# A fused top-k attention and feed-forward kernel: later transposes of a first head, earlier requests for the first low weights, more weight bits in the output banks, and new planner numbers

## The chip, the cores and the metric

The kernel runs on one core of one Trainium2 chip. The metric is the device time of one execution in microseconds (us), the median of the runs shown. Its engines are PE (TensorE, matrix products, with PEld for its weight loads), DVE (VectorE), ACT (ScalarE), POOL (GpSimd) and SP, whose queue issues the transfers (SPq in the rows).

## The reference

```python
# 8 batches, 8 heads, 576 positions, 64 wide
scores = q @ k.T / sqrt(64)
kth = np.partition(scores, -32, axis=-1)[..., -32:-31]      # 32nd largest of each row
scores = np.where(scores >= kth, scores, -1e9)
attn = softmax(scores)                                       # with 1e-9 added to the sum
x = (attn @ v).transpose(0, 2, 1, 3).reshape(4608, 512)
h = x @ w_in                                                 # 512 x 2048
P = a0 + a1*h + a2*h**2 + a3*h**3
Q = 1 + |b0|*|h| + |b1|*h**2
out = (P / (Q + 1e-6)) @ w_out                               # 2048 x 512
```

`w_in` and `w_out` are given with 64 bits, the rest with 32.

## The kernel before

**Attention.** The work is cut into 288 tiles. A tile is 128 query rows of one head against all 576 keys; a main unit is two such tiles, the two heads of a pair `hp` (there are four pairs, 0 to 3) at one block of rows, and the last 64 rows of both heads of a pair make one mixed tile. For a tile PE makes the scores `s` (`scores`, lines 706, 711 and 715), ACT copies them to `sb` (`evacuate`, 722), DVE folds the two halves into `hi` and `lo` and works through the largest values with MAX8 and MATCH_REPLACE8 (733 to 752), ACT makes the exponentials `e` (783), and DVE makes the masked product `pr` (`probs`, 786). PE then transposes `pr` (`trp`, 863) with the reciprocal sums `rw` (865), ACT copies the transposes to `p` (875), PE multiplies them with the values (`av`, 889), and ACT and POOL write the scaled result to `x_m` (906, 908). In `add_values`, `t0` and `t1` are the masked products of a unit's first and second head; transpose 0 needs only `t0`, transposes 1 and 2 need `t1`.

**Exact products from halves.** Most products are made of a high part and a low part of each operand. For the keys of a head pair this means one load `kl`, a high part `kh`, a low part, and four copies by the SP queue into `ka` and `kb` (606); for the queries one load `qx`, the two parts, and a stack of six copies into `q` (655, 657). Head pair 0 of batch 0 is "plain": its keys and queries are used as they are loaded (711).

**Feed-forward.** 256 rows of x are a chunk, 18 chunks in all, each of 8 groups. A group makes 24 products `ph` of 256 columns (1036) from `xh`, `xl`, the resident high weights `win_h` and the low weights `wi`, 512 KB that the SP queue fetches anew for each group (`load_wi`, 1044). ACT, POOL and DVE form the rational function, and 12 products `po` of 512 columns (1182) add to the output with `wout` and the low weights `wl` (1193). Names carry the batch or chunk: `wi_m_0_0` belongs to a main chunk.

**Weights.** In the first 230 us the 64-bit weights are also turned into high and low parts, 32 blocks of 512 columns. Each block takes two PSUM banks for its bits one after the other (lines 421 to 433): for blocks 0 to 7 of the two "o" banks, later the accumulators of `po`, for the others of the two "mm" banks, which the transposes, `av` and `ph` use as well.

**What sets the order.** `Plan` is a list scheduler that runs when the program is built. Every step has a priority key (smaller first), a length, the steps it waits for and the buffers it takes; keys are a tile's number times `T` plus an offset from the table `KEY` (for instance `AV` for `av`, `PT` for transposes, `WL` for the fetches of low weights). On the chip every engine and the SP queue then run their instructions strictly in the order that the plan wrote down, each waiting for its own semaphores.

Of the kernel before, what the change touches and what calls it, by code (L numbers as in the profile page):

```python
# [10 lines left out]
F32 = mybir.dt.float32  # L11
# [6 lines left out]
AX = mybir.AxisListType  # L18
PSUM = bass.MemoryType.PSUM

KEY = {'STAY': 0.0, 'WH': ('ACT', 'POOL'), 'XH': ('POOL',), 'TH': 0, 'EU': 4.119, 'SC': 0, 'HW': 256, 'Q0': ('POOL', 'ACT'), 'Q1': ('POOL',), 'SPLIT': (0, 1, 2, 3, 4, 5, 6, 7), 'XS': 1, 'P1': ('ACT', 'POOL'), 'P3': ('ACT', 'POOL'), 'RH': ('POOL',), 'p2': ('POOL', 'DVE'), 'p4': ('POOL',), 'ratio': ('POOL', 'DVE'), 'ratio_low': ('POOL',), 'URG': -100.0, 'PT': -10.303, 'AV': 2.038, 'MOE': 125.127, 'QT': -12.596, 'KT': -22.066, 'EL': 1.0, 'LOOK': 0.27, 'T': 5.448, 'KL': -16.348, 'KH': -8.844, 'PJ': 101.114, 'WL': 0.96, 'EX': 8.711, 'EW': 9.121, 'ALT': {'ACT': 0.388, 'DVE': 29.071, 'POOL': 0}, 'WG': 5.531, 'QL': -17.951, 'QH': 0.956, 'PACE': 15.382, 'B4': 0, 'RT': 1.0, 'WI': 0, 'WO': 0, 'MS': 0.313, 'NM': ('POOL', 'ACT'), 'WD': ('ACT',), 'LP': ('POOL',), 'FL': ('DVE',), 'VL': -15.549, 'RI': 7.085, 'ROOM': {'s': 1, 'e': 1, 'mm': 2, 'o': 2, 'k': 4, 'kr': 1, 'km': 2, 'q': 2, 'qr': 1, 'v': 2, 'sb': 3, 'lo': 1, 'hi': 2, 'pr': 2, 'p0': 1, 'p1': 1, 'p2': 1, 'm': 3, 'u': 4, 'rw': 1, 'fl': 2, 'x': 2, 'xm': 1, 'xs': 1, 't': 14, 'ob': 4, 'wi': 2, 'wl': 4}, 'TN': 2, 'IL': 0.996, 'SLACK': {'DVE': 0.0, 'PE': 0.0, 'ACT': 0.0, 'POOL': 0.0}, 'CF': 5.0, 'LD': 1.5, 'CL': 1.0, 'C0': 6.0, 'ML': 0.431, 'GL': 0.285}
NEG = -3.0e38
NB = 8

# [12 lines left out]
class Plan:  # L37
# [11 lines left out]
    BACK = 0.17  # L49
    CHANGE = 0.085  # L50
    SPARE = 2
    CLOCK = ((150.0, 1.2), (300.0, 1.05))

    def __init__(self, room):
        self.ring = {t: [-1.0] * n for t, n in room.items()}
# [134 lines left out]
def tile_topk_attention__then__rational_ffn(  # L190
# [10 lines left out]
    nc = tc.nc  # L201
# [31 lines left out]
    def add(*args, **kwargs):  # L233
        return plan.add(*args, **kwargs)
# [322 lines left out]
    def add_weights(key0, gap):  # L557
        n = 0
        blocks = []
        for e in range(0, DFF, 512):  # L560
            for c in range(HP):
                away = [win_l[e // 256 + i][:, c] for i in range(2)]
                split = (win_h[:, c, e : e + 512], None, away)
                tags = ["xs"] if c == HP - 1 and e < DFF // 2 else ["t"] * 3
                blocks.append((("i", c, e // 512), w_in, c * P, e, split, tags))
            for f in range(4 * (e // 512), 4 * (e // 512) + 4):
                split = (wout[f], None, [wout_l[f]] if f in wout_l else None)
                tags = ["t"] * (3 if f // FG in SPLIT else 2)
                blocks.append((("o", f), w_out, f * P, 0, split, tags))
        for n, (name, *args) in enumerate(blocks):  # L570
            bits = name[2] >= 4 - KEY["WI"] if name[0] == "i" else name[1] >= 16 - KEY["WO"]
            w_steps[name] = weight_block(*args, key0 + n * gap, f"w{n}", bits, "o" if n < 2 * HP else "mm")

    def add_kv(bi, hp, index, key):
        nm = f"{bi}_{hp}"
        kv = Obj()
        kv.index, kv.nm = index, nm
        kv.khold, kv.mhold = Hold("k", 2 * NJ), Hold("km")  # L580
        rhold = Hold("kr")
        kv.plain = index == 0

        def load_plain():
            kv.x = buf(kv.khold, [P, S], F32, f"ka_{nm}", "a")
            nc.sync.dma_start(kv.x, qk[index][:, 0:S])

        def load():
            kv.low = buf(rhold, [P, S], F32, f"kl_{nm}", "l")
            nc.sync.dma_start(kv.low, qk[index][:, 0:S])  # L590

        def high_part():
            kv.high = buf(rhold, [P, S], F32R, f"kh_{nm}", "h")
            affine(kv.high, kv.low, 1.0, 0.0)

        def low_part():
            engine().tensor_tensor(
                out=kv.low.bitcast(F32R), in0=kv.low, in1=kv.high.bitcast(F32), op=ALU.subtract
            )

        def stack():
            kv.k = [buf(kv.khold, [P, S], F32R, f"k{x}_{nm}", f"{x}") for x in "ab"]
            top, end = slice(0, D), slice(D, P)
            high, low = kv.high.bitcast(F32), kv.low
# [23 lines left out]
    def add_q(u):  # L628
        kv, key, pair = u.kv, u.key, u.pair
        n = len(pair.units) * P  # L630
        nm = f"{kv.nm}_{u.j}"
        q = pair.q = Obj()
        q.hold, rhold = Hold("q", 2 * len(pair.units)), Hold("qr")

        def load_plain():
            q.x = buf(q.hold, [P, 2, 2, 2 * P], F32, f"q_{nm}")[:, 0, 0]
            nc.sync.dma_start(q.x[:, 0:n], qk[kv.index][:, S + u.j * P :][:, 0:n])

        def load():
            q.x = buf(rhold, [P, 2, 2 * P], F32R, f"qx_{nm}")  # L640
            nc.sync.dma_start(q.x[:, 1, 0:n].bitcast(F32), qk[kv.index][:, S + u.j * P :][:, 0:n])

        def high_part():
            affine(q.x[:, 0, 0:n], q.x[:, 1, 0:n].bitcast(F32), 1.0, 0.0)

        def low_part():
            x = q.x.bitcast(F32)
            engine().tensor_tensor(out=q.x[:, 1, 0:n], in0=x[:, 1, 0:n], in1=x[:, 0, 0:n], op=ALU.subtract)

        def stack():  # L650
            q.q = buf(q.hold, [P, 2, 2, 2 * P], F32R, f"q_{nm}")
# [179 lines left out]
    def add_values(u):  # L831
# [190 lines left out]
    def add_group(x, o, g, key, split, xs, oholds):  # L1022
# [210 lines left out]
    def build():  # L1233
# [167 lines left out]
```

## Time and profile before

| what | value |
|---|---|
| runs of the kernel | 1501.80, 1502.86, 1498.61 us (median 1501.8) |
| the profiled execution | 1500.79 us, of which the span is 1498.9 us |
| busy share of the span | PE 93%, DVE 90%, ACT 85%, POOL 80% |
| mean granted TensorE clock | 0.965 of full |
| transfers | 301.57 MB, 201 GB/s on average |

Busy shares are averages over stages with different limits: at the start DVE works alone at speed, then PE and DVE are both nearly full, and at the end DVE has nothing left. So the stages have to be read one by one.

### The profile page before, as it was taken

What the parts mean: (1) busy time and instruction counts of PE and PEld (TensorE: products, weight loads), DVE (VectorE), ACT (ScalarE), POOL (GpSimd) and SP (SyncE); (2) the same over time, 40 slices, a digit from 0 to 9 for tenths busy, and PEclk for the clock granted to TensorE, in tenths of its full rate; (3) what the DMA queues carried; (4) which work ended last, traced back from release to release, by engine and by line L of the source; (5) the groups of instructions that cost most, each with busy time, mean ns of one, the idle gap of its engine ahead of it and who ended that gap; (6) DMA issues with size and microseconds to landing.
All of it is one profiled execution on the core that took longest, in us unless ns stands there. A gap on an engine that the chain in (4) does not pass through costs nothing.

```text
span 1498.9 us, 32412 instructions
## 1 busy us (share of the span) xinstructions
PE 1400.6 (93%) x9729; PEld 1178.6 (79%) x9729; DVE 1356.2 (90%) x4567; ACT 1274.5 (85%) x2592; POOL 1197.0 (80%) x1776
## 2 busy tenths in 40 slices
PE   5467789999999899999999999999999999999997
PEld 3345567878888788888888888888888788888886
DVE  7998999999999899999999999999999999999100
ACT  7776998989897798988898899899889798989664
POOL 6986889788877687888787788689777798877896
PEclk9656899999999999999999999999999999999999
DMA  7767885667765777567755676667765766564464
GB/s 227 230 202 220 239 253 179 195 182 215 233 198 144 221 207 237 166 203 226 222 184 174 213 235 200 195 192 221 216 205 151 241 204 223 157 197 144 142 219 135
DMA packets 173690, 301.57 MB, mean 201 GB/s; under 512 B 26048, under 2 KB 79296, under 8 KB 173504
## 3 DMA queue, kind: packets, MB, share of 16 engines
q1 hardware_dynamic: 173504, 299.39, 64.7%
q8 instruction: 80, 1.31, 0.4%
q14 instruction: 106, 0.87, 0.2%
HBM read 229.64 MB, written 18.87 MB: 166 GB/s over the span
## 4 chain that ended last, share of the span: by engine, by line
PE 74%; DVE 8%; ACT 6%; POOL 5%; issue 3%; DMA 2%; SPq 1%; POOLq 0%; ACTq 0%; DVEq 0%
PE ph_m L1036 21%; PE po_m L1182 19%; PE av L889 10%; PE s L715 8%; PE trp L863 7%; PE ph_t L1036 3%; DVE m L744 3%; PE po_t L1182 2%; DVE hi L752 2%; PE s L706 2%; DVE pr L786 1%; DMA wi_m<-win_l 1%; ACT p L875 1%; ACT sb L722 1%; PE trp L865 1%
## 5 line engine op out<-in xcount | busy, mean ns | idle before, releaser
L744 DVE MAX8 m<-hi 128x8 f32<-128x288 f32 (+1 forms) x1152 | 500.5, 452 | 0.4
L752 DVE MATCH_REPLACE8 hi<-m,hi 128x288 f32<-128x288 f32 x864 | 379.1, 443 | 0.0
L1036 PE MATMUL ph_m<-xh_m,win_h 128*128 128x256 f32 x1024 | 306.8, 300 | 4.6 <-ACT p L875 2.8
L1036 PE MATMUL ph_m<-xh_m,wi_m 128*128 128x256 f32 x1024 | 291.4, 285 | 6.3 <-DMA wi_m<-win_l 6.3
L1036 PE MATMUL ph_m<-xl_m,win_h 128*128 128x256 f32 x1024 | 289.8, 283 | 0.0
L875 ACT COPY p<-trp 128x512 f32<-128x512 f32 (+1 forms) x448 | 227.3, 513 | 43.1 <-PE trp L863 29.7
L863 PE MATMUL trp<-ident,pr 128*128 128x128 f32 x1312 | 224.0, 283 | 37.6 <-ACT w_w L433 20.6
L722 ACT COPY sb<-s 128x576 f32<-128x576 f32 x288 | 184.5, 641 | 59.3 <-PE s L715 37.5
L783 ACT ACTIVATE e<-sb,st 128x576 f32<-128x576 f32 x288 | 216.8, 753 | 18.9 <-DVE pr L786 15.4
L786 DVE SCALAR_TENSOR_TENSOR pr<-sb,m,e 128x576 f32<-128x576 f32 x288 | 229.7, 798 | 1.7 <-ACT e L783 1.0
L1092 POOL TENSOR_TENSOR pa_m<-pa_m,va_m 128x512 f32<-128x512 f32 x128 | 165.1, 1291 | 75.9 <-ACT va_m L1089 70.4
L863 PEld LDWEIGHTS trp<-ident,pr 128*128 128x128 f32 x1312 | 164.6, 145 | 72.9 <-ACT w_w L433 27.4
L1182 PE MATMUL po_m<-wout,g_m 128*128 128x512 f32 x512 | 218.2, 426 | 0.2
L1182 PE MATMUL po_m<-wl_m,g_m 128*128 128x512 f32 x512 | 202.4, 395 | 4.0 <-DMA wl_m<-wout_l 3.3
L1036 PEld LDWEIGHTS ph_m<-xh_m,win_h 128*128 128x128 f32 x1024 | 195.0, 190 | 13.4 <-ACT p L875 8.2
L1182 PE MATMUL po_m<-wout,gl_m 128*128 128x512 f32 x512 | 202.2, 395 | 2.5 <-POOL gl_m L1098 2.5
L1036 PEld LDWEIGHTS ph_m<-xh_m,wi_m 128*128 128x128 f32 x1024 | 194.6, 190 | 7.4 <-DMA wi_m<-win_l 7.4
L1036 PEld LDWEIGHTS ph_m<-xl_m,win_h 128*128 128x128 f32 x1024 | 195.3, 191 | 1.9
L889 PE MATMUL av<-p,vm 128*64 128x256 f32 (+1 forms) x1920 | 188.2, 345 | 3.8 <-ACT p L875 2.0
L1111 POOL TENSOR_TENSOR pa_m<-pa_m,hh_m 128x512 f32<-128x512 f32 x128 | 165.3, 1291 | 16.4 <-ACT hh_m L1117 6.5
L1098 POOL TENSOR_TENSOR gl_m<-pa_m,g_m 128x512 fp32r<-128x512 f32 x128 | 165.2, 1291 | 7.2 <-PE po_t L1182 3.0
L889 PEld LDWEIGHTS av<-p,vm 128*64 128x64 f32 x1920 | 112.2, 143 | 73.1 <-issue 17.7
(117 smaller groups left out, 3202.9 us busy)
## 6 DMA issues: line engine op xcount, KB each, us to landing
wl_m<-wout_l SPq DMA_DIRECT2D x256, 256.0 KB, 3.4
wi_m<-win_l SPq DMA_DIRECT2D x128, 512.0 KB, 4.1
vm<-in_v_dram SPq DMA_DIRECT2D x96, 320.0 KB, 3.1
q<-qx SPq DMA_DIRECT2D x124, 128.0 KB, 2.7
q<-qx SPq DMA_DIRECT2D x248, 64.0 KB, 2.1
km<-in_qk_dram SPq DMA_DIRECT2D x32, 352.0 KB, 3.7
kl<-in_qk_dram SPq DMA_DIRECT2D x31, 288.0 KB, 4.0
w_w<-in_moe_w_in_dram SPq DMA_DIRECT2D x32, 256.0 KB, 3.9
```

Of the source, the lines that this page charges most:

```text
L722: nc.scalar.copy(t.sb, t.s[:, :, 0:HF])
L744: nc.vector.max(to, t.both if not full and o == 24 else getattr(t, src))
L752: nc.vector.match_replace(x, t.m[:, o : o + 8], x, NEG)
L783: nc.scalar.activation(t.e, t.sb, AF.Exp, scale=SCALE, bias=t.st)
L786: nc.vector.scalar_tensor_tensor(out=t.pr, in0=t.sb, scalar=t.kth, in1=t.e, op0=ALU.is_ge, op1=ALU.mult, accum_out=u.ss[:, t.h : t.h + 1],)
L863: nc.tensor.transpose(u.ps[i][:, c * P : (c + 1) * P], u.pr[:, x], ident)
L875: nc.scalar.copy(pair.pT[i][:, at].rearrange("p c n -> p (c n)"), u.ps[i][:, 0 : n * P])
L889: nc.tensor.matmul(pair.av[d, 0 : u.nq * len(pair.units)], lhs, x[:, 0, d] if u.mixed else x[:, 0] if lone else x, start=(c == 0), stop=(c ...
L1036: nc.tensor.matmul(y.ph[:, f * NT : (f + 1) * NT], w, z[:, c, :], start=(c == 0 and i == 0), stop=(c == HP - 1 and i == 2),)
L1098: engine().tensor_tensor(out=tile_("gl", F32R), in0=y.pa, in1=y.g.bitcast(F32), op=ALU.subtract)
L1111: nc.gpsimd.tensor_tensor(out=x, in0=x, in1=z, op=ALU.mult)
L1182: nc.tensor.matmul(o.po[i], z, w, start=(ff == 0 and n == 0), stop=(ff == NF - 1 and n == 2),)
```

## The change

The table `KEY` gets new numbers and four pieces of code change. The numbers that the prediction speaks of: `AV` 2.038 to 4.464 and `PT` -10.303 to -7.135 (`av` and transposes yield more to scores), `WL` 0.96 to 21.38 (fetches of low weights yield more), `EX` 8.711 to 14.43, `EW` 9.121 to 19.62, `T` 5.448 to 5.373, `PACE` 15.38 to 17.42, `WG` 5.531 to 5.914 (time between weight blocks); `XH` lets ACT as well as POOL make high parts. New entries are `OB` 16, `K0` 50.97 and `W0` 108.17. The diff of the code:

```diff
-    CLOCK = ((150.0, 1.2), (300.0, 1.05))
+    CLOCK = ((150.0, 1.5), (210.0, 1.1))
...
-            w_steps[name] = weight_block(*args, key0 + n * gap, f"w{n}", bits, "o" if n < 2 * HP else "mm")
+            w_steps[name] = weight_block(*args, key0 + n * gap, f"w{n}", bits, "o" if n < KEY['OB'] else "mm")
...
-        kv.plain = index == 0
+        kv.plain = False
...
-        if kv.plain:
-            kv.load = add("SP", dma(1, P * S), load_plain, key=k2, take=[kv.khold])
-            return kv
+        if index == 0:
+            raw = Obj()
+            raw.khold, raw.plain = kv.khold, True
+            kv.first = raw
+            kv.khold.users = 4
+            raw.load = add("SP", dma(1, P * S), load_plain, key=k2, take=[kv.khold])
+            kv.khold = Hold("k", 2 * NJ - 4)
+            k2 += KEY['K0']
...
             for h, here, there in ((0, top, end), (1, end, top)):
-                nc.sync.dma_start(x[here, :, h, 0:n], y[here, :, 0:n])
-                for i in range(2):
-                    nc.sync.dma_start(x[there, i, h, 0:n], y[here, 1 - i, 0:n])
+                for rows in (here, there):
+                    nc.sync.dma_start(x[rows, :, h, 0:n], y[here, :, 0:n])
...
-        u, kv, key = t.u, t.u.kv, t.key
+        u, key = t.u, t.key
+        kv = u.kv.first if u.plain else u.kv
...
-            dep = [t0 if i == 0 else t1]
+            dep = [t1]
...
-        wi = add("SP", dma(1, P * 1024), load_wi, wdep + split[0:1], key + KEY['WL'], take=[wih])
+        wi = add("SP", dma(1, P * 1024), load_wi, wdep + (split[0:1] if x.n or g > 1 else []), key + KEY['WL'] - (KEY['W0'] if x.n == 0 else 0), take=[wih])
...
+            u.plain = n < 2
```

So transpose 0 waits for the second head's masked product too; the stack of queries takes four copies in place of six (the same bytes); the bits of blocks 8 to 15 use the "o" banks; the first chunk's low weights are asked for earlier, in the first two groups without waiting for the chunk itself; and only the first two units are plain, so head pair 0 of batch 0 loads its keys a second time and splits them.

How the new plan moves instructions is seen in three places. The first is PE's queue from the first tile of head pair 1 on (`s_0_1_0`); before it reads

```order
L715 MATMUL s_0_1_1_408<-kb_1_258,q_1_0_210 128x288 x4
L863 MATMUL trp_0_1_0_427<-ident,pr_1_0_300 128x128 x4
L863 MATMUL trp_0_1_0_461<-ident,pr_1_0_300 128x128
L865 MATMUL trp_0_1_0_461<-ident,rw_1_0_455 128x128
L889 MATMUL av_1_0_472<-p_0_0_0_235,vm_0_0_131 64x256
...
L889 MATMUL av_1_0_472<-p_0_0_0_342,vm_0_0_131 64x256 x2
L715 MATMUL s_1_1_0_514<-ka_1_257,q_1_0_210 128x288 x4
L863 MATMUL trp_0_0_1_524<-ident,pr_0_1_433 128x128 x4
```

and in the changed kernel

```order
L720 MATMUL s_0_1_1_398<-kb_1_231,q_1_0_269 128x288 x4
L868 MATMUL trp_0_1_0_425<-ident,pr_1_0_337 128x128 x4
L868 MATMUL trp_0_1_0_434<-ident,pr_1_0_337 128x128 x4
L868 MATMUL trp_0_1_0_470<-ident,pr_1_0_337 128x128
L870 MATMUL trp_0_1_0_470<-ident,rw_1_0_461 128x128
L720 MATMUL s_1_1_0_482<-ka_1_230,q_1_0_269 128x288 x4
L894 MATMUL av_1_0_494<-p_0_0_0_301,vm_0_0_131 64x256
...
L894 MATMUL av_1_0_494<-p_0_0_0_333,vm_0_0_131 64x256 x2
L720 MATMUL s_1_1_1_552<-kb_1_231,q_1_0_269 128x288 x4
```

The next tile's scores `s_1_1_0` now stand ahead of the block `av`, and both large transposes of a unit stand together behind its second head's scores.

The second is the SP queue around the fetch of `wi` for the fifth chunk (`wi_m_0_0`), some 490 us into the span; before

```order
L674 DMA vm_1_2_7119<-in_v_dram 128x640
L655 DMA q_2_2_7136<-qx_2_2_6972 64x2x256
L657 DMA q_2_2_7136<-qx_2_2_6972 64x256 x2
L655 DMA q_2_2_7136<-qx_2_2_6972 64x2x256
L657 DMA q_2_2_7136<-qx_2_2_6972 64x256 x2
L606 DMA ka_0_7181<-kh_0_5610 64x576
...
L606 DMA kb_0_7182<-kh_0_5610 64x576
L641 DMA qx_3_2_7216<-in_qk_dram 128x256
L1044 DMA wi_m_0_0_7221<-win_l_98 128x1024
```

and in the changed kernel

```order
L678 DMA vm_1_2_7101<-in_v_dram 128x640
L661 DMA q_2_2_7113<-qx_2_2_6942 64x2x256 x4
L606 DMA ka_0_7149<-kh_0_5509 64x576
...
L606 DMA kb_0_7150<-kh_0_5509 64x576
L646 DMA qx_3_2_7188<-in_qk_dram 128x256
L1198 DMA wl_m_2_7_1_7191<-wout_l_121 128x512
L1049 DMA wi_m_0_0_7203<-win_l_98 128x1024
```

The stack is two copies shorter, and a `wl` fetch now stands between it and `wi`.

The third is PE's queue where the first chunk's products begin; before

```order
L711 MATMUL s_3_0_0_1622<-ka_0_129,q_0_2_775 128x288 x2
...
L865 MATMUL trp_0_4_3_1675<-ident,rw_4_3_1611 128x128
L1036 MATMUL ph_m_0_0_1683<-xh_m_0_1415,win_h 128x256
L1036 MATMUL ph_m_0_0_1683<-xl_m_0_1416,win_h 128x256
```

and in the changed kernel

```order
L720 MATMUL s_3_0_1_1674<-kb_0_624,q_0_2_1006 128x288 x4
...
L720 MATMUL s_2_1_0_1755<-ka_1_230,q_1_2_1231 128x288 x4
L868 MATMUL trp_0_2_0_1776<-ident,pr_2_0_1577 128x128
L870 MATMUL trp_0_2_0_1776<-ident,rw_2_0_1761 128x128
L1041 MATMUL ph_m_0_0_1815<-xh_m_0_1388,win_h 128x256
L1041 MATMUL ph_m_0_0_1815<-xl_m_0_1389,win_h 128x256
```

The first `ph` moved behind two further score tiles (`s_3_0_1` and `s_2_1_0`). Counted over the whole queue, PE has this many `ph` and `po` ahead of a tile (before / changed): ahead of tile 32, 72 and 12 / 27 and 12; of tile 40, 138 and 48 / 105 and 33; of tile 64, 423 and 165 / 408 and 168; of tile 96, 768 and 375 / 768 and 369; of tile 240, 2496 and 1209 in both; behind the last `av`, 312 and 225 / 333 and 219.

## Rows read from the trace of the kernel before

**Rows 1.** The page: span, busy time and share with instructions, TensorE clock in tenths.
```profile
span 1498.9 us, 32412 instructions
PE 1400.6 (93%) x9729; PEld 1178.6 (79%) x9729; DVE 1356.2 (90%) x4567; ACT 1274.5 (85%) x2592; POOL 1197.0 (80%) x1776
PEclk9656899999999999999999999999999999999999
```

**Rows 2.** Busy time by stretch, with granted clock, share of transfers, GB/s.
```profile
core 0: us, PE busy (x) PEld busy (x) DVE busy (x) ACT busy (x) POOL busy (x), PEclk, DMA share, GB/s
0.00:100.00 100.00, 55.16 (x201) 34.69 (x202) 86.60 (x288) 75.71 (x190) 79.81 (x165) 0.77 0.71 220
100.00:163.00 63.00, 45.77 (x237) 29.67 (x235) 55.63 (x182) 47.28 (x119) 45.73 (x77) 0.64 0.73 224
163.00:200.00 37.00, 30.10 (x210) 24.76 (x208) 36.02 (x123) 34.41 (x76) 34.13 (x46) 1.00 0.80 235
501.00:1390.00 889.00, 880.86 (x6410) 757.24 (x6409) 878.03 (x2963) 789.40 (x1568) 713.06 (x1045) 1.00 0.65 201
1390.00:1498.90 108.90, 101.17 (x622) 88.54 (x620) 2.72 (x11) 67.81 (x113) 87.42 (x88) 0.98 0.53 168
```

**Rows 3.** Timeline of DVE: start, length, what, idle before it and its releaser.
```profile
7.45 0.46 DVE L733 TENSOR_TENSOR hi<-s,sb 128x288 f32<-128x288 f32 x1 [7.45 <-ACT sb L722]
...
17.45 0.46 DVE L733 TENSOR_TENSOR hi<-s,sb 128x288 f32<-128x288 f32 x1 [0.70 <-ACT sb L722]
...
40.95 0.46 DVE L733 TENSOR_TENSOR hi<-s,sb 128x288 f32<-128x288 f32 x1 [2.00 <-ACT sb L722]
...
64.43 0.46 DVE L733 TENSOR_TENSOR hi<-s,sb 128x288 f32<-128x288 f32 x1 [1.03 <-ACT sb L722]
...
88.43 0.46 DVE L733 TENSOR_TENSOR hi<-s,sb 128x288 f32<-128x288 f32 x1 [0.41 <-ACT sb L722]
...
140.92 0.46 DVE L733 TENSOR_TENSOR hi<-s,sb 128x288 f32<-128x288 f32 x1 [1.32 <-ACT sb L722]
```

**Rows 4.** Timeline of PE in the start: `av` ahead of scores, split and plain scores.
```profile
34.41 4.54 PE L889 MATMUL av<-p,vm 128*64 128x256 f32 x20
...
86.39 1.33 PE L715 MATMUL s<-ka,q 128*128 128x288 f32 x4
...
137.93 2.29 PE L711 MATMUL s<-ka,q 64*128 64x288 f32 x4
```

**Rows 5.** Waits, 0 to 165 us: engine, for whom, us in total, times, longest.
```profile
PE trp L863 <- ACT w_w L433: 16.1, 9, 3.0
```

**Rows 6.** Waits of PE, 165 to 1400 us.
```profile
PE ph_m L1036 <- DMA wi_m<-win_l: 6.3, 4, 2.9
...
PE po_m L1182 <- DMA wl_m<-wout_l: 3.3, 2, 1.7
```

**Rows 7.** Timeline of the SP queue ahead of one late `wi` (issue times).
```profile
482.24 0.33 SPq L674 DMA_DIRECT2D vm<-in_v_dram  x1
483.00 0.62 SPq L655 DMA_DIRECT2D q<-qx  x1
483.67 1.24 SPq L657 DMA_DIRECT2D q<-qx  x2
...
485.61 1.25 SPq L657 DMA_DIRECT2D q<-qx  x2
...
490.10 0.45 SPq L1044 DMA_DIRECT2D wi_m<-win_l  x1
```

**Rows 8.** Timeline of PE: the product that waited for this `wi`.
```profile
494.75 0.58 PE L1036 MATMUL ph_m<-xh_m,wi_m 128*128 128x256 f32 x1 [2.86 <-DMA wi_m<-win_l]
```

**Rows 9.** Busy time of the stretch behind that wait, columns as in rows 2.
```profile
494.00:501.00 7.00, 6.25 (x29) 6.23 (x30) 4.76 (x17) 1.96 (x5) 2.25 (x4) 0.51 0.73 253
```

**Rows 10.** The chain that ended last, its end: start, us, what.
```profile
1426.45 9.79 PE po_m L1182 x42
...
1444.75 5.76 PE ph_m L1036 x48
```

More of the change, by code (lines that the diff above doesn't have):

```diff
@@ L19 @@
 PSUM = bass.MemoryType.PSUM
-KEY = {'STAY': 0.0, 'WH': ('ACT', 'POOL'), 'XH': ('POOL',), 'TH': 0, 'EU': 4.119, 'SC': 0, 'HW': 256, 'Q0': ('POOL', 'ACT'), 'Q1': ('POOL',), 'SPLIT': (0, 1, 2, 3, 4, 5, 6, 7), 'XS': 1, 'P1': ('ACT', 'POOL'), 'P3': ('ACT', 'POOL'), 'RH': ('POOL',), 'p2': ('POOL', 'DVE'), 'p4': ('POOL',), 'ratio': ('POOL', 'DVE'), 'ratio_low': ('POOL',), 'URG': -100.0, 'PT': -10.303, 'AV': 2.038, 'MOE': 125.127, 'QT': -12.596, 'KT': -22.066, 'EL': 1.0, 'LOOK': 0.27, 'T': 5.448, 'KL': -16.348, 'KH': -8.844, 'PJ': 101.114, 'WL': 0.96, 'EX': 8.711, 'EW': 9.121, 'ALT': {'ACT': 0.388, 'DVE': 29.071, 'POOL': 0}, 'WG': 5.531, 'QL': -17.951, 'QH': 0.956, 'PACE': 15.382, 'B4': 0, 'RT': 1.0, 'WI': 0, 'WO': 0, 'MS': 0.313, 'NM': ('POOL', 'ACT'), 'WD': ('ACT',), 'LP': ('POOL',), 'FL': ('DVE',), 'VL': -15.549, 'RI': 7.085, 'ROOM': {'s': 1, 'e': 1, 'mm': 2, 'o': 2, 'k': 4, 'kr': 1, 'km': 2, 'q': 2, 'qr': 1, 'v': 2, 'sb': 3, 'lo': 1, 'hi': 2, 'pr': 2, 'p0': 1, 'p1': 1, 'p2': 1, 'm': 3, 'u': 4, 'rw': 1, 'fl': 2, 'x': 2, 'xm': 1, 'xs': 1, 't': 14, 'ob': 4, 'wi': 2, 'wl': 4}, 'TN': 2, 'IL': 0.996, 'SLACK': {'DVE': 0.0, 'PE': 0.0, 'ACT': 0.0, 'POOL': 0.0}, 'CF': 5.0, 'LD': 1.5, 'CL': 1.0, 'C0': 6.0, 'ML': 0.431, 'GL': 0.285}
@@ new lines @@
+KEY = {'OB': 16, 'K0': 50.96848245169408, 'W0': 108.17362977316282, 'STAY': 0.0, 'WH': ('ACT', 'POOL'), 'XH': ('POOL', 'ACT'), 'TH': 0, 'EU': 4.119, 'SC': 0, 'HW': 256, 'Q0': ('POOL', 'ACT'), 'Q1': ('POOL',), 'SPLIT': (0, 1, 2, 3, 4, 5, 6, 7), 'XS': 1, 'P1': ('ACT', 'POOL'), 'P3': ('ACT', 'POOL'), 'RH': ('POOL',), 'p2': ('POOL', 'DVE'), 'p4': ('POOL',), 'ratio': ('POOL', 'DVE'), 'ratio_low': ('POOL',), 'URG': -100.0, 'PT': -7.134778395148698, 'AV': 4.463837611760766, 'MOE': 125.23243066516059, 'QT': -12.596, 'KT': -22.066, 'EL': 1.0, 'LOOK': 0.540811001996511, 'T': 5.372682546626093, 'KL': -19.33166937506803, 'KH': -8.844, 'PJ': 103.53511744699887, 'WL': 21.377133033055376, 'EX': 14.425825290607323, 'EW': 19.61828985081265, 'ALT': {'ACT': 0.388, 'DVE': 29.071, 'POOL': 0}, 'WG': 5.913928207624261, 'QL': -17.188676077492165, 'QH': 0.956, 'PACE': 17.423649063765808, 'B4': 0, 'RT': 1.0, 'WI': 0, 'WO': 0, 'MS': 0.7404536167898788, 'NM': ('POOL', 'ACT'), 'WD': ('ACT',), 'LP': ('POOL',), 'FL': ('DVE',), 'VL': -13.67025212132888, 'RI': 7.085, 'ROOM': {'s': 1, 'e': 1, 'mm': 2, 'o': 2, 'k': 4, 'kr': 1, 'km': 2, 'q': 2, 'qr': 1, 'v': 2, 'sb': 3, 'lo': 1, 'hi': 2, 'pr': 2, 'p0': 1, 'p1': 1, 'p2': 1, 'm': 3, 'u': 4, 'rw': 1, 'fl': 2, 'x': 2, 'xm': 1, 'xs': 1, 't': 14, 'ob': 4, 'wi': 2, 'wl': 4}, 'TN': 2, 'IL': 1.3963475260244453, 'SLACK': {'DVE': 0.0, 'PE': 0.0, 'ACT': 0.0, 'POOL': 0.0}, 'CF': 5.0, 'LD': 1.5, 'CL': 1.0, 'C0': 6.0, 'ML': 0.44491012342883884, 'GL': 0.1789799677944829}
@@ L581, in add_kv @@
         rhold = Hold("kr")
-        kv.plain = index == 0
+        kv.plain = False
         def load_plain():
-            kv.x = buf(kv.khold, [P, S], F32, f"ka_{nm}", "a")
-            nc.sync.dma_start(kv.x, qk[index][:, 0:S])
+            kv.first.x = buf("k", [P, S], F32, f"ka_{nm}", "a")
+            nc.sync.dma_start(kv.first.x, qk[index][:, 0:S])
         def load():
@@ L654, in stack @@
             for h, here, there in ((0, top, end), (1, end, top)):
-                nc.sync.dma_start(x[here, :, h, 0:n], y[here, :, 0:n])
-                for i in range(2):
-                    nc.sync.dma_start(x[there, i, h, 0:n], y[here, 1 - i, 0:n])
-        if kv.plain:
+                for rows in (here, there):
+                    nc.sync.dma_start(x[rows, :, h, 0:n], y[here, :, 0:n])
+        if u.plain:
             q.load = add("SP", dma(1, P * n), load_plain, key=key + KEY['QL'], take=[q.hold])
@@ L664, in add_q @@
         s = add(two(n, *KEY['LP']), None, low_part, [s], key + KEY['QL'] + 1)
-        q.load = add("SP", 6 * dma(1, D * n), stack, [s], key + KEY['QL'] + 2, take=[q.hold], give=[rhold])
+        q.load = add("SP", 4 * dma(1, D * n), stack, [s], key + KEY['QL'] + 2, take=[q.hold], give=[rhold])
     def add_v(u):
```

## The prediction, made before the changed kernel ran

> **What bounds the kernel now.** I read the page first. PE is busy for 1400.6 us and DVE for 1356.2 us of a span of 1498.9 us, so neither share alone names the bound, and the clock line shows low tenths only in its first slices [rows 1]. Next come the stretches, which split the run in three [rows 2]. Up to 163 us PE is busy for 100.9 us at a mean clock of 0.64 to 0.77, and DVE for 142.2 us: here DVE leads, and each of its idle microseconds delays the tiles, since PE has time to spare. From 501 to 1390 us PE is busy for 880.9 and DVE for 878.0 of 889 us: both are full, and a wait of either that the other can't cover lengthens the run. After 1390 us DVE has nothing left and PE works off the remaining feed-forward.
>
> This gives the account that I use. The feed-forward products run back to back in the tail: 48 `ph` in 5.76 us and 42 `po` in 9.79 us, thus 0.120 and 0.233 us each [rows 10]. The total of products hardly changes. So the end moves by three things: how early the tiles come out of the start, how long PE and DVE wait in the full stretch, and how much product time is left behind the last `av`.
>
> The timeline of DVE shows the idle of the start. In 0 to 163 us it is 20.8 us, 7.4 of it ahead of the first tile [rows 3]. Five later folds of a new tile wait for `sb`, for 0.70, 2.00, 1.03, 0.41 and 1.32 us [rows 3]. The timeline of PE says why: at the lower clock level a block `av` takes 4.54 us [rows 4], and the next scores stand behind it. The wait table of the full stretch has only two entries worth counting: PE waits 6.3 us in four pieces for `wi` and 3.3 us in two for `wl` [rows 6]. The timeline of the SP queue shows how the longest comes about [rows 7]: a `vm` load is issued at 482.24 us, six copies of the query stack follow from 483.00 to 486.86 us, then the four key copies and `qx`, and `wi` is issued only at 490.10. Its product starts at 494.75 after a wait of 2.86 us [rows 8].
>
> **The change, part by part.**
>
> *Scores ahead of `av`, transposes together.* In the changed queue `s_1_1_0` stands ahead of the block `av`, and likewise in the next two pairs (the scores of heads 2 and 3, which the folds at 64.43 and 88.43 waited for); the first tiles' transposes no longer stand between two scores, which was the place of the 0.70 us. These four waits are 0.70 + 2.00 + 1.03 + 0.41 = 4.1 us [rows 3]. What is late instead is `av` itself, by one score of 1.33 us [rows 4]; behind it queue only `x_m` and the chunk's high and low parts, which PE uses some ten tiles later. In the full stretch waiting for `t1` costs nothing that I can find: transpose 1 of the same unit needed it anyway.
>
> *Fewer plain tiles.* Four tiles of head pair 0 become split. A plain score takes 2.29 us at the lower clock and a split one 1.33 us [rows 4], about 1.0 us less, and the fold at 140.92 us waited 1.32 us right behind a plain score [rows 3]. I count 1.0 us. The price is a second key load, four key copies and a few more for the queries: at 0.62 us an issue [rows 7] some 5 us of the SP queue, and two POOL instructions, spread over the first 110 us, where POOL is idle for 20 of 100 us [rows 2]. Hidden, I take zero; uncovered it would hold up a weight load, not a tile.
>
> So the start could gain 4.1 + 1.0 = 5.1 us. Other waits of the start keep their causes and may move, so I take 4.5. The bounds are 0, and 13.4 us, all idle of DVE up to 163 us but the first 7.4.
>
> *Output banks for blocks 8 to 15.* Transposes waited 16.1 us in nine pieces for ACT to free a bank from bits [rows 5]. A third of the 24 blocks that shared the "mm" banks leaves them. PE has slack there, so this pays only through scores queued behind a transpose, which are counted above: zero, with 2 us as the upper bound.
>
> *Two copies fewer in each query stack.* Six issues took 3.86 us [rows 7], 0.64 each, so four take 2.57 and what stands behind comes 1.29 us earlier. The timeline of the SP queue shows six `q` copies shortly ahead of the late fetch in each of the six waits of rows 6. Each can shrink by at most 1.29 us: 6 x 1.29 = 7.7 us. One of the six has a `wl` fetch put in between, and the larger `WL` pulls the other way, so I take 5. The bounds are -3 (a new wait like the longest) and 9.6 us, all of it [rows 6], with 3.1 us on top as follows.
>
> *The clock behind a long wait.* Behind the wait of 2.86 us the granted clock is 0.51 for 7 us, in which PE is busy for 6.25 us [rows 9]; at the full level the same products need half, so the fall cost 3.1 us more. If the wait shrinks to 1.6 us the fall may stay away; I leave it out of the sum. The Trainium skill, "TensorE: Matmul & The Clock Gate" (section "Why this matters for your kernels"), says that idle gaps between bursts of products put the clock back to its half rate. The trace agrees at this place with its 0.51, and by the rule alone one would add those 3.1 us to the gain if the gap closes.
>
> *The first low weights earlier, the first products later.* `W0` puts the request far ahead, but the first `ph` does not follow: it moves behind two more scores. Product time ahead of tile 32 falls from 72 x 0.120 + 12 x 0.233 = 11.4 to 6.0 us, ahead of tile 40 from 27.7 to 20.3, so up to 7.4 us lie behind. By tile 64 it is 89.2 against 88.1, by tile 240 nothing, and behind the last `av` 91.0 against 89.9 us. PE has room to catch up: from 163 to 200 us it is busy for 30.1 of 37 us [rows 2]. So this costs 1.1 us at the end, between 0 and 7.4.
>
> *The rest.* High parts on ACT, the other keys: ACT is idle for 100 us of 889 in the full stretch [rows 2], so I take zero.
>
> **The sum.** 1498.9 - 4.5 - 5.0 + 1.1 = 1490.5 us of span. The profiled execution took 1500.79 us, 1.9 outside its span, which gives 1492.4; the median of the runs, 1501.8, lies 1.0 above that execution, so 1493.4 us.
>
> **The rivals.**
>
> *A. The forecast*, 1493 us, with a range of its own from 1487 to 1497.
>
> *B. No change.* Tiles leave the start earlier, but PE can't use it: from 501 us on it is busy for 99% of the time, so 5 us less in the start only turn into 5 us more waiting for PE, and of the fetches only the 1.29 us of the longest wait counts. For it speaks PE's 880.9 of 889 us; against it that PE had nothing but slack where the gain arises, and that the backlog of 1.1 us is small. Time: 1501.8 - 1.3 + 1.1 = 1501.6.
>
> *C. Slower, by the clock.* With 5.4 us less product time ahead of tile 32, TensorE stays longer at the lower level (1.2 GHz) past 163 us, where before it ran at 1.00 [rows 2]. Work there was 30.1 - 5.4 = 24.7 us in 37; at the lower level it takes 49.4, which is 12.4 us more than the stretch has, 0.34 us for each microsecond that the level lasts. The gains of 8.4 us are gone at 25 us, and at the full 37 the time is 1493.4 + 12.4 = 1505.8; should the 7.4 us of backlog stay too, 1512. For it speaks that up to 163 us the clock fell again and again under a like load (0.64 in the mean [rows 2]); against it that a PE with its queue full keeps the level: from 501 to 1390 us it is 1.00. The skill's rule above is the one that speaks against the change here: by it the later first burst leaves the gaps open longer, and the time would be this rival's.
>
> *D. More than forecast.* The start gains 9 us rather than 4.5, since `av` and plain scores hit more of it than the folds that I counted, and the full stretch 8 + 3.1. Time: 1493.4 - 4.5 - 6.1 = 1482.8. For it: DVE's idle of 13.4 us is there; against it: half of it stands at waits whose cause the change leaves alone.
>
> **How the numbers follow.** A has a chance of 0.47, B 0.25, C 0.14, D 0.14. The likeliest is A, so 1493.4 us. The range takes in D, B and the lower part of C: 1482 to 1505, and about 2 in 10 is left out (C above 1505, D below 1482, and what I have not thought of). A difference of 0.3%, 4.5 us, is about what a measurement of this kernel tells from no change: faster is under 1497.3, slower over 1506.3. A and D are faster, 0.61, B with the lower part of C the same, 0.27, the rest of C slower, 0.12.
>
> **What would show it.** In the changed kernel's trace the folds of tiles 4 to 14 should wait less than 1 us in all for `sb`, and DVE's idle up to 163 us should be 14 to 17 us. The fetch behind a stack should be issued about 1.3 us sooner after its `vm`, and PE's waits for `wi` and `wl` should sum to some 4 to 5 us. The clock should reach and keep 1.00 by 175 us; if it does so only after 200 us, C holds. PE behind DVE's last instruction should work about 1 us longer. I am wrong if waits for low weights grow through `WL`, or if DVE gets its idle back behind new waits between 100 and 230 us, where the weight bits still share the "mm" banks.

## The result, and the profile after

The changed kernel takes 1483.5 us (median of 1483.46, 1483.61, 1484.09 and 1482.73) against 1500.2 us before in the same comparison, a ratio of 0.9892 [0.9876, 0.9908]. It gained 16.7 us, where 8.4 were forecast (from 1501.8, the median of the first three runs before; against that it is 18.3). The profiled execution took 1483.46 us, with this page (as in [rows 1]):

```profile
span 1481.4 us, 32234 instructions
PE 1388.4 (94%) x9729; PEld 1178.2 (80%) x9729; DVE 1353.0 (91%) x4567; ACT 1297.7 (88%) x2616; POOL 1183.8 (80%) x1756
PEclk9766899999999999999999999999999999999999
```

The stretches of [rows 2], in the changed kernel:

```profile
core 0: us, PE busy (x) PEld busy (x) DVE busy (x) ACT busy (x) POOL busy (x), PEclk, DMA share, GB/s
0.00:100.00 100.00, 54.70 (x211) 35.32 (x211) 89.69 (x304) 80.10 (x200) 81.02 (x165) 0.82 0.81 247
100.00:163.00 63.00, 43.38 (x259) 31.50 (x259) 62.05 (x208) 55.63 (x139) 50.89 (x85) 0.72 0.79 246
163.00:200.00 37.00, 25.99 (x170) 21.58 (x169) 34.76 (x116) 31.87 (x73) 30.93 (x46) 0.91 0.74 217
501.00:1390.00 889.00, 884.60 (x6438) 761.65 (x6437) 867.23 (x2931) 803.56 (x1575) 710.24 (x1039) 1.00 0.66 200
1390.00:1481.40 91.40, 84.12 (x504) 74.33 (x502) 0.42 (x2) 56.41 (x93) 72.82 (x70) 0.97 0.55 174
```

Up to 163 us DVE is busy for 151.7 us where it was 142.2. From 163 to 200 us the clock is 0.91 and no longer 1.00. To see where the time came from I follow the tiles. The timeline of DVE gives the start of the masked product `pr` of the 49th tile, before

```profile
275.64 0.80 DVE L786 SCALAR_TENSOR_TENSOR pr<-sb,m,e 128x576 f32<-128x576 f32 x1
```

and after

```profile
264.92 0.80 DVE L791 SCALAR_TENSOR_TENSOR pr<-sb,m,e 128x576 f32<-128x576 f32 x1
```

So the tiles leave the start 10.7 us earlier; I call this the lead. The last `pr` starts at 1391.2 before and 1374.9 after, 16.2 us earlier, so the full stretch adds 5.5. Behind it the kernel before works for 107.7 us and the changed one for 106.5, another 1.3 (rounded from finer figures). Together this is the 17.5 us of the span: **start 10.7, full stretch 5.5, end 1.3**. The forecast had 4.5, 5.0 and -1.1.

DVE's waits in 0 to 165 us (engine, for whom, us in total, times, longest), before

```profile
DVE hi L733 <- ACT sb L722: 14.0, 8, 7.4
DVE w_w_b L427 <- ACT w_w_b L421: 3.4, 4, 1.4
DVE ss L841 <- POOL ss L281: 1.7, 1, 1.7
```

and after

```profile
DVE hi L738 <- ACT sb L727: 7.9, 2, 7.2
DVE cf L552 <- POOL cf L484: 1.6, 1, 1.6
DVE w_w_b L427 <- ACT w_w_b L421: 0.2, 1, 0.2
```

Without the first tile's wait the folds lose 0.7 us in place of 6.6. The 3.4 us of weight bits and the 1.7 us for `ss` are gone as well, and 0.9 us more for `cf` came. These waits alone don't make up the lead. In the stretch from the start to the 49th `pr` (us, DVE busy, then the granted clock, the share and the rate of transfers), before and after,

```profile
0.00:275.64 275.64, 253.30 (x843) 0.83 0.72 223
0.00:264.92 264.92, 250.66 (x844) 0.85 0.76 231
```

DVE idles for 22.3 and 14.3 us: 8.0 of the 10.7 are idle time. The other 2.7 are busy time, for as many instructions. By the timeline of DVE their lengths add up to 1.2 us more than before, but neighbours overlap by 58.9 us in all in place of 55.0, in 823 pairs in place of 805. Fewer waits leave more pairs that overlap; why they overlap by more as well stays open. PE's waits for transfers in 165 to 1400 us [rows 6] are now

```profile
PE po_m L1187 <- DMA wl_m<-wout_l: 1.8, 1, 1.8
PE ph_m L1041 <- DMA wi_m<-win_l: 0.5, 1, 0.5
```

2.3 us in place of 9.6. SP's queue ahead of the `wi` of [rows 7]:

```profile
472.53 0.33 SPq L678 DMA_DIRECT2D vm<-in_v_dram  x1
473.29 2.57 SPq L661 DMA_DIRECT2D q<-qx  x4
...
479.11 0.44 SPq L1198 DMA_DIRECT2D wl_m<-wout_l  x1
479.59 0.43 SPq L1049 DMA_DIRECT2D wi_m<-win_l  x1
```

From `vm` to `wi` it takes 7.06 us where it was 7.86, although a `wl` fetch stands between now. And the chain that ended last closes with products of the same length as in [rows 10], 0.120 and 0.232 us each:

```profile
1454.45 2.88 PE ph_m L1041 x24
1457.33 16.69 PE po_m L1187 x72
```

### The profile page after: what moved, and what is told of

Same layout as the page of the kernel before. It is cut to its first block, busy times and chain, and to the rows that moved or that the text cites. A ratio compares the mean times of both kernels' runs of the same rounds, so it can differ in the third digit from the quotient of the medians.

```text
span 1481.4 us, 32234 instructions
## 1 busy us (share of the span) xinstructions
PE 1388.4 (94%) x9729; PEld 1178.2 (80%) x9729; DVE 1353.0 (91%) x4567; ACT 1297.7 (88%) x2616; POOL 1183.8 (80%) x1756
## 4 chain that ended last, share of the span: by engine, by line
PE 80%; DVE 6%; ACT 5%; POOL 4%; DMA 2%; issue 2%; SPq 1%; POOLq 0%; DVEq 0%; ACTq 0%
PE ph_m L1041 23%; PE po_m L1187 21%; PE av L894 10%; PE s L720 8%; PE trp L868 8%; PE ph_t L1041 3%; PE po_t L1187 3%; DVE m L749 2%; DVE hi L757 2%; PE s L711 2%; ACT p L880 1%; DVE pr L791 1%; PE trp L870 1%; ACT sb L727 1%; POOL cf L484 1%
## 5 line engine op out<-in xcount | busy, mean ns | idle before, releaser
L788 ACT ACTIVATE e<-sb,st 128x576 f32<-128x576 f32 x288 | 217.0, 754 | 12.2 <-DVE pr L791 7.6
```

The source lines that it names most:

```text
L788: nc.scalar.activation(t.e, t.sb, AF.Exp, scale=SCALE, bias=t.st)
```

## The experiments

All times are medians; each ratio is against the kernel before on the same chip. Lead, full stretch and end are the account above for the profiled execution, as us earlier (-) or later (+) than before; its own time stands in the column "profiled" and can differ from the median by up to 7 us (the kernel before: 1500.8). Beside these groups of runs the kernel before had medians from 1499.7 to 1501.4 us, so I estimate that a difference of medians between groups is good to some 1.5 us.

| kernel | us | ratio [95%] | profiled | lead | full | end |
|---|---|---|---|---|---|---|
| changed | 1483.5 | 0.9892 [0.9876, 0.9908] | 1483.5 | -10.7 | -5.5 | -1.3 |
| e1_six_copies | 1502.6 | 1.0007 [0.9991, 1.0023] | 1506.7 | -7.7 | +15.0 | -1.3 |
| e2_four_copies | 1491.9 | 0.9935 [0.9912, 0.9957] | 1492.3 | -0.1 | -8.5 | -0.1 |
| e3_old_numbers | 1502.1 | 1.0008 [0.9995, 1.0021] | 1500.8 | +0.7 | -1.7 | +1.2 |
| e4_new_numbers | 1513.3 | 1.0088 [1.0063, 1.0114] | 1506.2 | +0.4 | -2.8 | +7.9 |
| e5_first_head | 1492.8 | 0.9951 [0.9934, 0.9968] | 1490.0 | -5.9 | -4.7 | -0.2 |
| e6_banks_8 | 1489.5 | 0.9938 [0.9920, 0.9957] | 1489.6 | -8.4 | -3.7 | +1.0 |
| e7_all_plain | 1497.1 | 0.9983 [0.9970, 0.9996] | 1495.2 | -7.1 | -2.6 | +3.9 |
| e8_low_late | 1494.5 | 0.9959 [0.9941, 0.9976] | 1494.2 | -7.0 | -1.1 | +1.6 |
| n1_gap_after | 1492.9 | 0.9955 [0.9938, 0.9971] | 1490.3 | -3.8 | -5.6 | -1.3 |
| n2_pace_after | 1489.1 | 0.9925 [0.9909, 0.9942] | 1489.4 | -6.5 | -5.9 | +1.0 |
| n3_pace_before | 1501.5 | 1.0005 [0.9992, 1.0017] | 1501.6 | +0.5 | +0.7 | -0.3 |
| n4_first_term | 1507.8 | 1.0043 [1.0028, 1.0057] | 1509.3 | +4.5 | +0.6 | +3.5 |
| f1_gap_before | 1505.0 | 1.0027 [1.0017, 1.0037] | 1509.8 | +1.5 | +5.0 | +2.6 |
| f2_pace_before | 1514.7 | 1.0097 [1.0073, 1.0121] | 1514.8 | +0.4 | +3.5 | +10.1 |
| f4_eight_copies | 1525.5 | 1.0160 [1.0142, 1.0178] | 1525.8 | +0.4 | +24.9 | -0.3 |
| f5_six_pace | 1508.9 | 1.0065 [1.0043, 1.0088] | 1505.9 | -7.7 | +11.5 | +1.0 |
| g1_gap_before_four | 1498.7 | 0.9988 [0.9978, 0.9998] | 1501.9 | +4.0 | -5.9 | +2.6 |
| g2_pace_before_four | 1504.4 | 1.0030 [1.0014, 1.0045] | 1505.0 | +2.6 | -6.7 | +8.4 |

### The copies of the query stack, with the order of every queue kept

The planner's length of the step stays as it was, so only the copies themselves differ.

```diff
 e1: changed kernel          e2: the reverse, in the kernel before
-                for rows in (here, there):
-                    nc.sync.dma_start(x[rows, :, h, 0:n], y[here, :, 0:n])
+                nc.sync.dma_start(x[here, :, h, 0:n], y[here, :, 0:n])
+                for i in range(2):
+                    nc.sync.dma_start(x[there, i, h, 0:n], y[here, 1 - i, 0:n])
```

> The changed kernel with the stack of queries in six copies again; the order of every queue is kept, only the two copies more stand in it. Theory S (my term of 5 us: a fetch of low weights behind a stack comes 1.29 us earlier for two copies less): 2 to 5 us slower than the changed kernel, 1485.5 to 1488.5, with the waits of PE for wi and wl in 165 to 1400 us up from 2.3 to 5 us or more. Rival (the longer leads of the new numbers have removed these waits anyway): 1483.5, waits unchanged, DVE's idle up to 163 us unchanged at 11.

> The kernel before with four copies per stack of queries, everything else and the order of every queue as before. Theory S: its waits for wi and wl fall from 9.6 to 2 to 5 us, the fall of the clock behind 494 us goes, and the time is 4 to 8 us below before, 1492 to 1496. Rival (the fetches wait for something else, a buffer or their place in the queue): 1500, waits above 8 us.

Both came out beyond theory S: two copies fewer save 9.5 us in the old order (1501.4 to 1491.9) and two more cost 19.1 in the new one. The rows of all engines' waits in 300 to 1400 us show the place. The kernel before:

```profile
DVE hi L733 <- ACT sb L722: 10.3, 13, 2.4
PE ph_m L1036 <- DMA wi_m<-win_l: 6.3, 4, 2.9
POOL qx L281 <- DMA qx<-in_qk_dram: 4.9, 5, 1.4
PE po_m L1182 <- DMA wl_m<-wout_l: 3.3, 2, 1.7
```

e2, the same order with four copies:

```profile
DVE hi L732 <- ACT sb L721: 3.1, 8, 0.7
PE ph_m L1035 <- DMA wi_m<-win_l: 1.9, 1, 1.9
PE po_m L1181 <- DMA wl_m<-wout_l: 1.2, 2, 0.6
POOL qx L281 <- DMA qx<-in_qk_dram: 0.8, 2, 0.5
```

The changed kernel:

```profile
DVE hi L738 <- ACT sb L727: 4.4, 9, 1.7
POOL qx L281 <- DMA qx<-in_qk_dram: 2.1, 3, 1.2
```

and e1, its order with six:

```profile
DVE hi L739 <- ACT sb L728: 21.7, 25, 2.0
POOL qx L281 <- DMA qx<-in_qk_dram: 14.2, 13, 1.6
PE ph_m L1042 <- DMA wi_m<-win_l: 10.0, 8, 2.2
PE po_m L1188 <- DMA wl_m<-wout_l: 4.5, 2, 2.7
```

PE's waits for `wi` and `wl` go from 9.6 to 3.1 us in e2 and from 2.3 to 14.5 in e1, as I had reasoned. I had not counted that a PE held up there also holds up the scores behind it: DVE's waits for `sb` follow, 10.3 to 3.1 and 4.4 to 21.7. By the timelines 13.9 of e1's 21.7 us stand within 12 us behind such a wait of PE; for the rest this cause is not shown. DVE's idle time between the 49th and the last `pr` is 14.3 us before, 7.0 in e2, 9.4 in the changed kernel and 28.1 in e1, which is all but 0.6 to 1.2 us of the column "full". The fall of the clock behind 494 us is not gone in e2 but shorter, 3.4 us in place of 6.8. One of e1's falls of the clock in this stretch, 3.4 us at half from 1169.3 us on, stands behind such a wait (2.67 us for a `wl`, by the timeline of PE).

Then the dose, eight copies in the order of before:

```diff
-                nc.sync.dma_start(x[here, :, h, 0:n], y[here, :, 0:n])
                 for i in range(2):
+                    nc.sync.dma_start(x[here, i, h, 0:n], y[here, i, 0:n])
                     nc.sync.dma_start(x[there, i, h, 0:n], y[here, 1 - i, 0:n])
```

> The kernel before with eight copies in each stack of queries in place of six, the same bytes, the order of every queue kept. If the time goes with the number of issues on SP's queue, two more cost about what two fewer saved, 8 to 12 us: 1508 to 1513, with waits of PE for wi and wl well above 9.6. If four copies only removed single late fetches, two more cost as much as my account of 1.29 us a fetch allows, 3 to 6 us: 1503 to 1507.

It took 24.3 us more, twice the upper end of the first view: four, six and eight copies stand at -9.5, 0 and +24.3. Waits of f4 in the same stretch (16 of PE's waits for weights in place of 6, and 21.9 of the 24.3 us of `hi` within 12 us behind one of them):

```profile
DVE hi L733 <- ACT sb L722: 24.3, 20, 4.2
POOL qx L281 <- DMA qx<-in_qk_dram: 16.1, 10, 3.3
PE ph_m L1036 <- DMA wi_m<-win_l: 12.6, 6, 4.8
PE po_m L1182 <- DMA wl_m<-wout_l: 11.0, 8, 3.0
```

A rival is that the transfers themselves grow, and not the issues. The pages of e2, before and f4 (queue, packets, MB, time of the packets as a share of 16 engines' span) speak against it:

```profile
q1 hardware_dynamic: 171520, 299.38, 65.7%
q1 hardware_dynamic: 173504, 299.39, 64.7%
q1 hardware_dynamic: 175488, 299.40, 63.8%
```

Each further copy adds 16 packets under 512 B, 1.1% at each step, and the packets' time is 979, 970 and 972 us: it does not grow with the copies.

### Numbers without code, code without numbers

e3 is the changed code with the old table `KEY` (and `OB`, `K0`, `W0`) and the old `CLOCK`; e4 is the old code with the new table and `CLOCK`.

> The changed code (four copies, 16 blocks in the output banks, two plain units, transpose 0 behind the second head, early low weights) with the planner numbers of before. Theory N (the start's gain of some 10 us is that of the order that the new numbers give): DVE's idle up to 163 us goes back to 18 to 21 us and the time is 1492 to 1496, since only the stack's part stays. Theory C (the gain is that of the code pieces: banks free of weight bits, cheaper scores): idle 11 to 14 us, time 1483 to 1487.

> The code of before (six copies, 8 blocks in the output banks, all of head pair 0 plain, transpose 0 behind its own head, low weights as before) with the new planner numbers. Theory N: DVE's idle up to 163 us falls to 11 to 14 us and the time is 1488 to 1492, the stack's part missing. Theory C: idle stays at 18 to 21 us, time 1497 to 1502.

Neither theory holds: the idle is 19.4 and 19.2 us, the lead +0.7 and +0.4, and e3's time of 1502.1 us lies above both ranges, e4's 1513.3 too. Neither the numbers nor the code alone gives the start's gain. A mere re-ordering is in both of them as well, but the nudged orders below keep 3.8 and 6.5 us of the lead, and these two none. DVE's waits in 0 to 165 us, e3

```profile
DVE hi L738 <- ACT sb L727: 12.1, 5, 7.3
DVE ss L846 <- POOL ss L281: 2.6, 1, 2.6
DVE w_w_b L427 <- ACT w_w_b L421: 2.4, 3, 1.1
```

and e4

```profile
DVE hi L733 <- ACT sb L722: 11.5, 6, 7.1
DVE w_w_b L427 <- ACT w_w_b L421: 4.4, 3, 3.2
```

The folds still wait 4.8 and 4.4 us behind the first, and the waits for bits are back.

### One piece undone, and controls that undo nothing

```diff
 e5:
-            dep = [t1]
+            dep = [t0 if i == 0 else t1]
 e6: 'OB': 8 in place of 16
 e7:
-            u.plain = n < 2
+            u.plain = u.bi == 0 and u.hp == 0 and not u.mixed
 (and no second load and split of these keys)
 e8:
-  ... wdep + (split[0:1] if x.n or g > 1 else []), key + KEY['WL'] - (KEY['W0'] if x.n == 0 else 0), take=[wih])
+  ... wdep + split[0:1], key + KEY['WL'], take=[wih])
 n1: changed kernel, 'WG' 5.85 in place of 5.914
 n2: changed kernel, 'T' 5.39 in place of 5.373
```

> The changed kernel with transpose 0 waiting for its own head alone again; numbers and the rest as changed. Theory T (my first term: transposes together, out of the way between two scores, save the start's waits): fold waits behind the first come back from 0.7 to 3 us or more, DVE's idle up to 163 us 14 to 18, time 1487 to 1491. Theory B (the banks do it) and P (the split tiles do it): idle stays near 11, time 1482 to 1486, as far as the plan keeps its order elsewhere.

> The changed kernel with the bits of blocks 8 to 15 in the two mm banks again. Theory B (the output banks free the transposes from weight bits; I had costed them at nothing): waits of transposes for bits go back to some 10 us or more, DVE waits for w_w_b for 3 us or more, the start's lead shrinks by 4 us or more, time 1488 to 1495. Theories T and P: waits of PE for bits come back, but under its slack; DVE's idle up to 163 us stays near 11, time 1482 to 1486.

> The changed kernel with all eight main tiles of head pair 0 of batch 0 plain again, without the second load of its keys and their split. Theory P (a split score takes about half of a plain one at the lower clock, and I counted 1 us for it): the start's lead falls by 3 us or more around 110 to 145 us, time 1487 to 1492. Theories B and T: at most 1 us lost, 1483 to 1485.

> The changed kernel with the first chunk's low weights asked for as before (behind the chunk's own parts and without W0). If the early request matters: the first products come later, PE waits for wi once or twice more around 200 us, and the time is 2 to 5 us longer, 1486 to 1489. If not, as I had costed it: 1482 to 1485.

> A control: the changed kernel with the time between weight blocks WG at 5.85 in place of 5.914, a number with no cost of its own; it re-orders the queues from about the eleventh tile on. If the start's lead and the time come from the mechanisms of the change, it keeps both: lead over before at 300 us of 8 us or more, time 1482 to 1487. If they hang on this one order of instructions, it is as slow as the kernels with one piece undone: lead 5 to 8 us, 1489 to 1497.

> A second control: the changed kernel with 5.39 in place of 5.373 as the time of a tile, which leaves the first tiles' order as it is and re-orders the queues from about 125 us on. By the mechanisms: 1482 to 1487. By the one order: 1489 to 1497.

Each undone piece costs 6.0 to 13.6 us, which looks like four proofs. The controls take that away: numbers moved by 1.1% and 0.3%, which cost nothing by themselves, cost 9.4 and 5.6 us. So e5, e6 and e8 (9.3, 6.0, 11.0) can't be told from a mere re-ordering, and e7 (13.6) loses no more than a nudge of the kernel before does below (f2, 13.5). The leads of e5 to e8, -5.9 to -8.4, lie between those of the controls, -3.8 and -6.5, or above them: no single piece is shown to carry the start.

The waits named beforehand say the same. Behind the first tile the folds wait 2.5, 2.0, 1.8 and 0.8 us for `sb` in e5 to e8, and 1.2 and 1.0 in the controls, where the changed kernel has 0.7 and before 6.6. DVE's idle up to 163 us is 12.2 to 14.6, in the controls 16.6 and 13.0. In e6 the transposes wait for bits again, 17.6 us where the changed kernel has 3.4, yet DVE's own wait for bits is 1.6 of the 3.4 us that it had before, and the lead shrinks by 2.3, no more than a control's. In e8 the first `ph` starts at 123.4 us, earlier than the changed kernel's 137.5 and not later, and no wait for `wi` stands between 165 and 300 us; so its loss has not the cause that was named for it.

### The first term alone, and controls of before

n4 is the kernel before with `dep = [t1]` and the new `AV` and `PT`. n3 and f2 have 5.43 and 5.41 for `T`, f1 has 5.47 for `WG`; g1 and g2 are f1 and f2 with four copies, and f5 is n2 with six, order kept.

> The kernel before with my first term alone: transpose 0 waits for the second head, and AV and PT have the new numbers; everything else as before. By my term: the fold waits behind the first tile fall from 6.6 to 2.5 us, 4.1 us less, and the time is 1496 to 1498. If the folds' waits take the banks and the split tiles as well: they fall by 2 us or less, or others of DVE take their place, and the time is 1500 or more.

n4's folds wait 13.5 us, 5.7 without the first, and the tiles come 4.5 us late. The term alone gives nothing that shows beyond a re-ordering.

> A third control: the kernel before with 5.43 in place of 5.448 as the time of a tile; a few hundred rows of a queue are re-ordered. Expected: within 3 us of before. If more, a re-ordering alone is worth as much as a piece of the change.

> The kernel before with 5.47 in place of 5.531 as the time between weight blocks, as in the control of the changed kernel; it re-orders the queues from about the sixteenth tile on. If only the changed kernel stands in a lucky order, this takes before's time, 1498 to 1504. If before's own order was picked as finely as the changed one, this is slower by as much as the changed kernel's controls were, 1506 to 1511.

> The kernel before with 5.41 in place of 5.448 as the time of a tile, which re-orders more than the first control of before did. As for the one above: 1498 to 1504, or 1506 to 1511.

n3, with few rows moved, stays at before; f1 and f2 are slower by 3.9 and 13.5 us. So before stands better than two of its three neighbours that were run, as the changed kernel does than both of its own. I call the order of either kernel as it stands the picked one, and compare picked with picked and nudged with nudged.

> The second control of the changed kernel (5.39 as the time of a tile) with six copies in a stack again, its order kept. If the cost of the two copies is one of SP's queue whatever the order, it is 10 us or more above that control's 1489: 1499 to 1508. If the 19 us that they cost the changed kernel come of its one order, it is 5 us or less: 1490 to 1494.

> The nudged kernel of before with 5.47 as the time between weight blocks (1505.0 us), its order kept, with four copies in a stack. It fills the last cell of a square: old or new numbers and pieces, six or four copies. If the two copies are worth the same everywhere in old orders: 9 us less, 1494 to 1498, and all the rest of the change is then worth 3 to 7 us beside the changed kernel's controls at 1489.1 and 1492.9. If they are worth as much as in the new orders: 1484 to 1488, and the rest of the change is worth nothing.

> The nudged kernel of before with 5.41 as the time of a tile (1514.7 us), its order kept, with four copies in a stack. By the first view 1503 to 1507, by the second 1493 to 1497.

Two copies more cost 19.8 us on n2, and two fewer save 6.3 on f1 and 10.2 on f2 (by the ratios 1.40%, 0.39% and 0.67%). The square in medians (us):

| | six copies | four copies |
|---|---|---|
| old, picked order | 1501.4 | 1491.9 |
| old, nudged (f1, f2; g1, g2) | 1505.0, 1514.7 | 1498.7, 1504.4 |
| new, picked order | 1502.6 | 1483.5 |
| new, nudged (n1, n2; f5) | 1508.9 | 1492.9, 1489.1 |

In the old orders the two copies are worth 6 to 10 us, in the new ones 19 to 20. All the rest of the change is worth 8.4 us with four copies in the picked orders (5.8 and 15.3 in the nudged pairs), and with six copies nothing that shows: 1.2 us more in the picked order, between f1 and f2 in the nudged one.

## Why the prediction was wrong

The step that failed is **the term of the start**: "Other waits of the start keep their causes and may move, so I take 4.5." It measured 10.7. My sum over the folds came out right in size, by luck as the next paragraph shows: their waits behind the first tile fell by 5.9 us where I had counted 5.1, and tiles 4 to 14 wait less than 1 us as I wrote. But the other waits did not keep their causes. DVE's own wait for weight bits, 3.4 us, I had not looked at; I knew the bits only as a wait of transposes [rows 5] and costed the output banks at zero (e6, with a lead 2.3 us smaller, does not refute that zero; it is not the banks alone that took DVE's wait away). The bits' 3.2 us and the 1.7 for `ss` are another 4.9, less the 0.9 more for `cf`, and DVE's idle up to 163 us is 11.3 us, below the 14 to 17 that I named. The 2.7 us of DVE's busy time were not in my sum at all. Rival D, at 1482.8 us, gave about this time by luck: its start of 9 us is near, though not for its reason, but it had 11.1 for the full stretch and 1.1 us lost at the end.

The cause that I named for the folds fell. n4 made exactly that edit and the folds kept 5.7 of their 6.6 us; e3 and e4 kept 4.8 and 4.4; and e5, which takes the edit out of the changed kernel, brings 1.8 back. What removed them comes with the new order as a whole, which neither numbers nor code gave alone; which moves of it did so stays open. Of the 10.7 us, orders nudged by about 1% and 0.3% of one number keep 3.8 and 6.5; the rest belongs to the one order that was picked.

**The full stretch** came out at 5.5 us for 5.0, but as a net. The two copies alone give 8.5 in the order of before, near the 7.7 that I had counted for them ahead of the deductions. I had looked at PE's waits only; DVE's waits for `sb`, 7.2 us less in e2, move with them. The changed order by itself would have lost 15.0 us there with six copies (e1; its profiled execution lies 4.1 us above its median, so by the median it is about 11). Why the same two copies cost twice as much in it stays open: the time from a `wi` issue to its first product is no shorter (median 11.8 us in e1, 10.7 before, from the issues and products of the 300 to 1390 us timeline), so the larger `WL` is not shown to be the cause.

**The end** was forecast at +1.1 us and is -1.3, within what the controls scatter.

**The clock.** The fall of [rows 9] behind the long `wi` is gone, as rival D had it. Rival C's sign is there, but not its price:

```profile
172.90:179.70 6.80, 6.26 (x28) 6.04 (x29) 6.80 (x24) 4.34 (x10) 5.20 (x7) 0.50 0.64 183
203.60:207.00 3.40, 3.29 (x16) 2.89 (x15) 3.00 (x12) 3.15 (x7) 3.24 (x6) 0.50 0.83 258
```

These stretches (columns as in [rows 2]) are at half the full clock, and the first begins in a gap that the timeline of PE shows:

```profile
173.44 1.97 PE L868 MATMUL trp<-ident,pr 128*128 128x128 f32 x8 [3.57 <-ACT w_w L433]
```

After 207 us the clock stays full to the last microseconds. The low stretches between 163 and 207 us last 10.2 us, and the threshold that I gave for C was 25; DVE is busy for all 6.80 us of the first. Some is given back here all the same: the lead is 13.7 us at the 25th tile (its `pr` starts at 143.4 in place of 157.1) and 10.7 at the 49th, and DVE idles for 3.3 us from 163 to 300 us where it idled for 1.6. The Trainium skill, "TensorE: Matmul & The Clock Gate" (section "Why this matters for your kernels"), has gaps between bursts put the clock back, and the trace agrees with its 3.57 us gap; what it costs depends on whether DVE waits, and there it did not.

Rival B fell: PE could use earlier tiles, and the lead of 10.7 us at the 49th tile was 16.2 at the last.

## What to carry to other kernels

Count what an issue costs in the queue that also carries fetches just in time, and follow a delayed product to everything behind it in PE's order: here 124 to 126 copies fewer of the same bytes were the largest part that could be told from a re-ordering, 9.5 us in the order of before. When one table of numbers sets the order of everything, undoing a piece measures the piece and the re-ordering together. A nudge of a number that costs nothing by itself, or an edit that keeps every queue's order, is needed beside it before a loss is put down to the piece.

## What was not expected of the hardware

A copy from `qx` to `q` held SP's queue for 0.61 to 0.64 us in the mean whatever its size: 372 copies of 64 and 128 KB before at 0.64, 496 of 64 KB in f4 at 0.61, 252 of 128 KB after at 0.62, while the `wi` fetches of 512 KB took 0.38 to 0.42. So between 64 and 128 KB the bytes did not count, the issues did. And the queue was far from full: its issues sum to 660 us of before's 1499, 571 of e2's 1490 and 731 of f4's 1524. The Trainium skill, "Perfetto Trace Analysis" (section "What "DMA-bound" means"), takes an issuing engine whose track is solid with DMA slices for the sign of a kernel bound by issuing. By that sign this queue, at 44%, would be no suspect; here it delayed PE all the same, since at that share bursts of six copies cost 9.5 us more than bursts of four, and bursts of eight 33.8.
